# A banded attention and two-layer MLP kernel: first weights on ScalarE's queue, w_out's halves between chunks of V, one group of transposes moved into the second product

## The chip, the cores and the metric

The kernel runs on one core of a Trainium2 chip. A core has five engines that run their own instruction streams and wait for each other by semaphores: TensorE (PE) for matmuls and transposes, VectorE (DVE), ScalarE (ACT), GpSimd (POOL), and SyncE (SP), which here only issues transfers. Sixteen DMA engines move the data. The metric is device time in microseconds; shown are the median of several runs, and the profile of one execution.

## The reference

Eight batches, eight heads, sequence 576, head size 64. Each query sees the keys at most 32 positions away; the result, laid out as 4608 tokens of 512 features, goes through a two-layer MLP with tanh-GELU.

```python
scores = scale * np.matmul(q, k.transpose(0, 1, 3, 2))
mask = np.abs(pos[:, None] - pos[None, :]) <= window      # window = 32
attn = softmax(np.where(mask, scores, -1e9))
x = np.matmul(attn, v).transpose(0, 2, 1, 3).reshape(4608, 512)
h = x @ w_in                                              # w_in: 512 x 2048
g = 0.5 * h * (1.0 + np.tanh(c * (h + 0.044715 * h * h * h)))
out = g @ w_out                                           # w_out: 2048 x 512
```

## The kernel before, in words

**Tiles.** The tokens are cut into nine tiles of 512. Tile t goes through the first product (`ffn_in`, L522, with the gelu at L549 on ACT) and the second product (`ffn_out_0`, L609, for tile 0 and `ffn_out`, L622, a scheme with seven half-size products, for the others). The attention of batch t+1 is worked in small pieces between the matmuls of tile t's second product, and leaves its result, transposed, in the ring `xT`, from which the next first product reads. Batch 0's attention has no product to hide in and runs alone at the start.

**Attention pieces.** Heads are worked in pairs, groups 0 to 3; group "-1" stands for the last tokens (tail) of the batch before. For a group: casts to fp16 (`cast_early`, L295), eight PE transposes of queries and keys into one PSUM buffer (`trans_pair`, L322) and copies from there to QT (L333, DVE) and KT (L334, DVE or ACT by an argument), scores (`score`, L417) with the exponential on ACT (L448), the band mask on DVE (L454), sums over keys by a product with ones (`sum_up`, L457), logarithm and exponential on ACT in place of a division (L494, L495, or L883, L885 for two groups at once), the product with V (`times`, L461), and the final multiplication into xT (`spread`, L498, at L504 or L510). V is needed twice, shifted by 64 keys; the second form is copied on DVE (`pair_chunk`, L196: lines L198 and L200; `pair_v`, L190, for batch 0). `trans_tails` (L312) turns the last 64 queries and keys, `cast_tails` (L307) casts them.

**PSUM buffers.** Score buffers have the tags S0 and S1; O, D, x0 and x1 are single banks. The last quarter of tile 0's first product keeps its results for columns 12 and 13 in S0 and for 14 and 15 in S1, so S0 is free once the second of the last four gelus has read it.

**Order.** It is written by hand: each engine executes its instructions in the order in which the program emits them, and waits in that order. Around tile 0's second product the order is a plan, `PLAN_0` (L53): before matmul number i of the 64, the actions listed at i are emitted (L848 to L911). The letter is the kind and the number the group, `@` names the score buffer:

- `r` transposes and copies, `s` scores and exponential, `m` mask, `k` casts of queries and keys on DVE
- `n` sums, logarithm and exponential for two groups, `v` sums, product with V and logarithm for one, `p` product with V for two, `x` the multiplication into xT
- `e` cast of a chunk of V on POOL, `d` its shifted copy on DVE, `t` transposes of batch 0's tail queries
- `w`, `u` casts of w_out (shared by DVE, ACT and POOL), `c` differences of w_out's blocks

Matmul i needs the block of w_out that `ORDER_0` (L64) gives: column blocks 0 to 3 for the first 16, and so on.

**Transfers.** Nearly all loads are issued by SP, in program order (L221 to L243 and L742 to L781). w_in comes in four blocks of 1 MB, in halves of 512 KB, w_out in the same manner; both go through five staging buffers (`stage_w`, L205) and are cast to fp16. V of batch 0 is loaded head by head (`v_of_pair`, L228, 128 KB each in pieces of 256 bytes). In the kernel before, SP issues three pairs of V heads, half of w_in's first block, one head, a quarter, the last head, a quarter, then the other blocks. ACT issues two loads at the very start (L222, L224).

**The first product of tile 0.** Block 0 of w_in at L755 to L767, then `quarter(1)`, `quarter(2)`, `quarter(3)` (L786 to L801), each of 16 matmuls followed by four gelus. In the middle of `quarter(3)` stands `trans_pair(1, 0)`, the transposes of batch 1's group 0, with the key copy on ACT. `load_table` (L97) changes ACT's function table.

Of the kernel before, what the change touches and what calls it, by code (L numbers as in the profile page):

```python
# [10 lines left out]
FP16 = mybir.dt.float16  # L11
# [25 lines left out]
def cut(b):  # L37
# [12 lines left out]

PLAN_0 = {4: "s0@0", 9: "r1@1", 14: "s1@0", 15: "w1", 16: "m0", 19: "k2", 22: "r2@1", 23: "m1", 25: "s2@0", 27: "t-1@1",  # L53
          29: "w2", 31: "s-1@1", 33: "n0@0", 35: "e0", 36: "m2", 37: "k3", 38: "w5", 39: "m-1", 40: "r3@1", 43: "e1",
          45: "s3@0", 46: "v-1@1 d0", 47: "w3 e2", 48: "m3", 50: "d1", 51: "n2@0 x-1", 52: "e3 e4 d2", 54: "d3 p0@0",
          55: "u3 p2@1 x0 x1", 56: "x2 x3", 60: "c1"}
PLAN_1 = PLAN | {10: "s0@0", 12: "s1@1", 33: "s2@0", 40: "v0@1 v1", 50: "x0", 53: "x1", 57: "s-1@1", 62: "s3@0 v2",
                 63: "m-1", 66: "m3", 73: "v-1@1", 76: "x2", 80: "x-1", 86: "v3", 90: "s4@1", 98: "m4"}
PLAN_1[16] = "m0 m1"
# [13 lines left out]
def kernel(  # L73
# [9 lines left out]
    nc = tc.nc  # L83
    B, H, S, D = q.shape
    DM, DF = moe_w_in.shape
    NTOK = B * S
    NPAIR = H // 2
# [117 lines left out]
    def stage_w():  # L205
        return stage.tile([128, 4, 512], FP32, name="wst", tag="stage")

    def load_w_in(i, w, c0=0, c1=4):
        nc.sync.dma_start(w[:, c0:c1, :], w_in_v[:, c0:c1, 512 * i:512 * i + 512])
        return w  # L210

    def load_w_out(i, w, c0=0, c1=4):
# [12 lines left out]
    qk(4)  # L225
    qk(6)
    load_table(exp_set)
    def v_of_pair(g, hs=(0, 1)):  # L228
        for h in (2 * g + x for x in hs):
            nc.sync.dma_start(raws[0][3][:, :, h, :], v[0, h, 0:512, :].rearrange("(c p) d -> p c d", p=128))  # L230

    vs(4)
    for g in range(3):
        v_of_pair(g)
    wi = [stage_w()]
    load_w_in(0, wi[0], 0, 2)
    for x in range(2):
        v_of_pair(3, (x,))
        load_w_in(0, wi[0], 2 + x, 3 + x)
    for i in range(1, 4):  # L240
        wi.append(stage_w())
        for c0 in (0, 2):
            load_w_in(i, wi[i], c0, c0 + 2)  # L243

    idle = KTs[1][:, 0, 0:512]
    nc.vector.memset(idle, 0.0)
# [470 lines left out]
    cast_early(0, 3, split)  # L717
    turn(2)
    score(0, 1, 1)
    trans_out(0, 2, *pts[2])  # L720
    cast_vt(0)
    spin(1)
# [46 lines left out]
    cast_w(wi[2], w_in16[:, :, 1024:1536], (0, 2))  # L769
    wo.append(load_w_out(1, stage_w()))  # L770
    qk(4)
    tails_0("q")
    wo.append(load_w_out(2, stage_w(), 0, 2))
    qk(6)
    vs(0)
    load_w_out(2, wo[2], 2, 4)
    vs(1)
    wo.append(load_w_out(3, stage_w(), 0, 2))
    vs(2, 3, 4)
    load_w_out(3, wo[3], 2, 4)  # L780
    tails()  # L781

# [13 lines left out]
    band_out()  # L796
    quarter(2, 0, 1, 2, 3)
    cast_early(1, 0, split)
    quarter(3, 0, 1)
    trans_pair(1, 0, psO.tile([128, 8, 128], FP16, name="pt", tag="D"), bank16(0)[:, 0:4, :], copy=nc.scalar.copy)  # L800
    quarter(3, 2, 3)  # L801
    load_table(exp_set)
    cast_w(wo[0], w_out16[:, 0:4, :], (0,), (0, 2, 3, 1))
    cast_early(1, 1, (nc.vector, nc.vector))
# [8 lines left out]
    for t in range(NT):  # L813
        b = t + 1
        att = b < B
        if t:
            for fc in range(begun):
                ffn_in(t, fc, 3, 4, then=False)
            for fc in range(begun):
                gelu(t, fc)  # L820
            if att and b > 1:
                parts = cast_and_turn(b)
            for fc in range(begun, NF):
                ffn_in(t, fc)
                if t == 1 and fc == 3:
                    parts[0]()
                    combine(4, nc.vector)
                if t == 1 and 6 <= fc < 10:
                    cast_v(2, fc - 6)
                if t == 1 and 9 <= fc < 14:  # L830
                    parts[1](fc - 9)
                if t == 1 and fc == 8:
                    trans_tails(1, psO.tile([128, 8, 128], FP16, name="pt", tag="O"))
                if t == 2 and fc in (8, 9):
                    store(0, *later[1 if fc == 8 else 3])
                if t > 1 and fc == 8 and att:
                    pair_v(b, nc.vector.tensor_copy)
        plan = PLAN_0 if not t else PLAN_1 if t == 1 else PLAN if att else {5: "v-1", 31: "x-1"} if t == B - 1 else {}

        def group(g):  # L840
            return (b, g) if g >= 0 else (b - 1, 4)

        if plan and t:
            load_table(exp_set)
        if t and b + 1 < B:
            load_qk(b + 1)
        ods = {}
        for i in range(113 if t else 65):  # L848
            if t and i == (4 if t > 1 else 46) and b + 1 < B:
                nc.gpsimd.tensor_copy(after, KLs[b % 2][:, 3, 0:1])  # L850
                load_v(b + 1)
            for act in plan.get(i, "").split():
                kind, at = act[0], int(act[act.index("@") + 1:]) if "@" in act else None
                g = int(act[1:].split("@")[0])
                if kind == "w":
                    if g == 3:
                        cast_w(wo[g], w_out16[:, 12:16, :], cs=(0, 1), on_dve=(0,))
                    else:
                        cast_w(wo[g % 3], w_out16[:, 4 * (g % 3):4 * (g % 3) + 4, :], on_act=(1, 3),
                               cs={1: range(4), 2: (0, 1), 5: (2, 3)}[g])  # L860
                elif kind == "e":
                    cast_vt(1) if g == 4 else cast_v(1, g)
                elif kind == "k":
                    cast_early(1, g, (nc.vector, nc.vector))
                    if g == 2:
                        cast_tails(0, nc.gpsimd, even)
                elif kind == "t":
                    trans_tails(0, spare(at)[0], even)
                elif kind == "r":
                    trans_pair(1, g, *spare(at), copy=nc.scalar.copy if g == 2 else nc.vector.tensor_copy)  # L870
                elif kind in "np":
                    pair = psS.tile([128, 2, 512], FP32, name="ps_od", tag=f"S{at}")
                    for x in range(2):
                        if kind == "n":
                            sum_up(1, g + x, pair[:, x, :], groups[(1, g + x)])
                        else:
                            ods[g + x] = (pair[:, x, :], lts[g + x])
                            times(1, g + x, pair[:, x, :], groups.pop((1, g + x)))
                    if kind == "n":
                        n = size(1, g)  # L880
                        lts[g], lts[g + 1] = lt4[:, g, :], lt4[:, g + 1, :]
                        for x in range(2):
                            nc.scalar.activation(lts[g + x][:, 0:n], pair[:, x, 0:n], AF.Ln)  # L883
                        for x in range(2):
                            nc.scalar.activation(lts[g + x][:, 0:n], lts[g + x][:, 0:n], AF.Exp, scale=-1.0)  # L885
                elif kind == "u":
                    cast_w(wo[g], w_out16[:, 12:16, :], on_act=(3,), cs=(2, 3))
                    cast_tails(1, nc.gpsimd)
                    load_qk(2)
                elif kind == "c":  # L890
                    if g == 1:
                        B12 = combine_w()
                    combine(g, nc.vector)
                elif kind == "s":
                    score(*group(g), at)
                    if t == 1 and g == 4:
                        load_table(gelu_set)
                elif kind == "d":
                    pair_chunk(b, g, nc.vector.tensor_copy)
                elif kind == "m":  # L900
                    mask(*group(g))
                elif kind == "v":
                    bb, gg = group(g)
                    o, d = weigh(bb, gg, at)
                    ods[g] = (o, invert(bb, gg, d))
                    if t and g < 0 and b + 1 < B:
                        load_vt(b + 1)
                    if t > 1 and g == (3 if att else -1):
                        load_table(gelu_set)
                else:  # L910
                    spread(*group(g), *ods[g])  # L911
            if t == 1 and i == 30:
                cast_vt(2)
                store(0, *later[0])
                store(0, *later[2])
            if t == 1 and i in PAIR_1:
                pair_v(2, nc.vector.tensor_copy, PAIR_1[i])
            if t == 0 and i < 64:
                ffn_out_0(*ORDER_0[i])
            elif t and i < 112:  # L920
                ffn_out(t, i)
        if t == 0:
            wino_rest(B12)
            load_table(gelu_set)
        else:
            ffn_last(t)
        begun = 3 if t < NT - 1 else 0
        for fc in range(begun):
            ffn_in(t + 1, fc, 0, 3)
# [28 lines left out]
```

## Time and profile before

| what | value |
|---|---|
| median of 5 runs | 302.14 us (301.98 to 306.6) |
| profiled execution: its own time | 301.98 us |
| its span, and granted TensorE clock | 300.2 us, 0.994 |
| PE busy | 288.8 us, 96% of the span |
| DVE busy, ACT busy, POOL busy | 196.1, 194.6, 90.7 us |
| chain that ended last | PE 83%, DVE 5%, ACT 4%, DMA 3% |
| moved by DMA | 50.73 MB, 169 GB/s on average |

The span runs from the first to the last instruction of the profiled execution; its own time is 1.8 us longer, and the comparison between kernels is by the runs' times. "Chain" is the work that ended last, followed back at each step to what released it. A row of the timeline gives start, length, engine, line, operation, what it writes and reads, and how often; brackets give idle time of that engine before it and what ended it. PE's ends are modelled and overlap: matmuls of 512 columns start every 0.216 us although each is listed with about 0.38 us.

### The profile page before, as it was taken

What the parts mean: (1) busy time and instruction counts of PE and PEld (TensorE: products, weight loads), DVE (VectorE), ACT (ScalarE), POOL (GpSimd) and SP (SyncE); (2) the same over time, 40 slices, a digit from 0 to 9 for tenths busy, and PEclk for the clock granted to TensorE, in tenths of its full rate; (3) what the DMA queues carried; (4) which work ended last, traced back from release to release, by engine and by line L of the source; (5) the groups of instructions that cost most, each with busy time, mean ns of one, the idle gap of its engine ahead of it and who ended that gap; (6) DMA issues with size and microseconds to landing.
All of it is one profiled execution on the core that took longest, in us unless ns stands there. A gap on an engine that the chain in (4) does not pass through costs nothing.

```text
span 300.2 us, 7125 instructions
## 1 busy us (share of the span) xinstructions
PE 288.8 (96%) x2893; PEld 179.8 (60%) x2893; DVE 196.1 (65%) x438; ACT 194.6 (65%) x307; POOL 90.7 (30%) x141
## 2 busy tenths in 40 slices
PE   7889999899999999999999999999999999999994
PEld 2534444445774488548854885478547864784583
DVE  4563567996969676967696669766876635442452
ACT  4865776679785695669567956695678666606600
POOL 3425416102537050605080506060700050015000
PEclk9979999999999999999999999999999999999999
DMA  7999999899899999898999996989692031004013
GB/s 214 223 302 384 371 300 253 230 191 212 197 217 193 245 221 171 147 136 209 182 170 162 228 162 148 151 212 175 99 185 37 3 102 40 2 7 134 2 37 103
DMA packets 116518, 50.73 MB, mean 169 GB/s; under 512 B 98007, under 2 KB 110039, under 8 KB 116486
## 3 DMA queue, kind: packets, MB, share of 16 engines
q1 hardware_dynamic: 87428, 37.88, 61.2%
q0 software_dynamic: 27936, 11.35, 25.5%
q10 hardware_dynamic: 1122, 1.06, 1.1%
q8 instruction: 22, 0.36, 0.5%
q14 instruction: 10, 0.08, 0.1%
HBM read 36.70 MB, written 9.44 MB: 154 GB/s over the span
## 4 chain that ended last, share of the span: by engine, by line
PE 83%; DVE 5%; ACT 4%; DMA 3%; issue 1%; SPq 1%; POOL 0%; POOLq 0%
PE mm L639 31%; PE mm L541 21%; PE ph L541 19%; PE ps_s L436 3%; PE ps_d L459 2%; PE ps_o L469 2%; ACT gT L549 2%; DMA vr<-in_v_dram 2%; DMA tr<-in_k_dram 2%; DVE xT L504 1%; PE py L613 1%; PE mm L613 1%; SPq L230 1%; PE ps_od L459 1%; PE ps_od L469 1%
## 5 line engine op out<-in xcount | busy, mean ns | idle before, releaser
L541 PEld LDWEIGHTS <-w_in 128*128 128x128 f16 x576 | 56.4, 98 | 66.6 <-issue 1.9
L541 PE MATMUL mm<-xT,w_in 128*128 128x512 f16 x304 | 75.2, 381 | 0.1
L549 ACT ACTIVATE gT<-mm 128x512 f16<-128x512 f32 x76 | 45.2, 598 | 40.0 <-PE mm L541 39.2
L541 PE MATMUL ph<-xT,w_in 128*128 128x512 f16 x272 | 68.8, 382 | 0.0
L603 POOL DMA_DIRECT2D out_dram<-y x55 | 33.4, 616 | 87.4 <-DVE y L668 75.1
L639 PEld LDWEIGHTS <-s 128*128 128x128 f16 x512 | 49.4, 98 | 6.0
L584 DVE TENSOR_TENSOR s<-gT 128x512 f16<-128x512 f16 x64 | 27.6, 431 | 36.9 <-ACT gT L549 36.9
L549 ACT ACTIVATE gT<-ph 128x512 f16<-128x512 f32 x68 | 38.0, 600 | 13.6 <-PE ph L541 13.6
L639 PE MATMUL mm<-t,s 128*128 128x256 f16 x376 | 45.0, 273 | 0.0
L639 PEld LDWEIGHTS <-gT 128*128 128x128 f16 x384 | 35.8, 98 | 6.7
L448 ACT ACTIVATE pe<-ps_s 128x960 f16<-128x960 f32 (+1 forms) x32 | 30.6, 977 | 12.5 <-PE ps_s L436 12.3
L639 PE MATMUL mm<-w_out,gT 128*128 128x256 f16 x256 | 33.2, 273 | 0.0
L98 ACT ACT_TABLE_LOAD x18 | 23.1, 1283 | 2.2 <-issue 1.9
L494 ACT ACTIVATE lt<-ps_d 128x480 f32<-128x480 f32 (+2 forms) x28 | 15.6, 556 | 10.6 <-PE ps_d L459 6.8
L495 ACT ACTIVATE lt<-lt 128x480 f32<-128x480 f32 (+3 forms) x36 | 21.1, 587 | 1.1
L469 PEld LDWEIGHTS <-V 128*64 128x64 f16 x520 | 14.3, 112 | 8.6 <-DVE V L194 2.1
L454 DVE TENSOR_TENSOR pe<-pe,band 128x960 f16<-128x960 f16 x28 | 18.2, 669 | 1.1 <-ACT pe L448 1.1
L184 POOL DMA_DIRECT2D V<-in_v_dram x20 | 17.9, 913 | 1.2 <-PE ps_s L436 0.4
L639 PE MATMUL mm<-t,gT 128*128 128x256 f16 x128 | 16.5, 273 | 0.0
L504 DVE TENSOR_TENSOR xT<-ps_o,lt 128x480 f16<-128x480 f32 (+5 forms) x26 | 13.5, 537 | 2.3 <-PE ps_o L469 2.3
L436 PE MATMUL ps_s<-QT,KT 64*64 64x128 f16 (+3 forms) x576 | 13.9, 216 | 0.8 <-ACT KT L334 0.5
L436 PEld LDWEIGHTS <-KT 64*64 64x64 f16 x576 | 10.1, 106 | 7.4 <-issue 4.2
(110 smaller groups left out, 324.8 us busy)
## 6 DMA issues: line engine op xcount, KB each, us to landing
kr<-in_k_dram SPq DMA_DIRECT2D x31, 256.0 KB, 10.5
qr<-in_q_dram SPq DMA_DIRECT2D x6, 1024.0 KB, 8.5
wst<-in_moe_w_in_dram SPq DMA_DIRECT2D x7, 512.0 KB, 8.4
V<-in_v_dram POOLq DMA_DIRECT2D x20, 128.0 KB, 8.7
wst<-in_moe_w_out_dram SPq DMA_DIRECT2D x2, 1024.0 KB, 11.3
wst<-in_moe_w_out_dram SPq DMA_DIRECT2D x4, 512.0 KB
qr<-in_q_dram SPq DMA_DIRECT2D x7, 256.0 KB, 6.9
out_dram<-y POOLq DMA_DIRECT2D x6, 192.0 KB, 6.2
```

What stands on the lines that cost most here:

```text
L98: nc.scalar.add_instruction(mybir.InstLoadActFuncSet(name=nc.get_next_instruction_name(), act_func_set_id=which, ins=[], outs=[]))
L184: nc.gpsimd.dma_start(V[:, c, :, :], v[b, :, 128 * c:128 * c + 128, :].rearrange("h p d -> p h d"))
L436: nc.tensor.matmul(ps[64 * half:64 * half + 64, h, 4 * n * r:4 * n * r + 4 * n].rearrange("k (j p) -> k j p", j=4)[:, :, p0 - q0:p1 - q0], ...
L448: nc.scalar.activation(pe, ps[:, :, 0:w], AF.Exp, scale=SCALE)
L454: nc.vector.tensor_tensor(pe, pe, m.rearrange("k (o j) p -> k o j p", o=1).broadcast_to(list(pe.shape)), op=ALU.mult)
L469: nc.tensor.matmul(o[64 * h:64 * h + 64, cols].rearrange("d (j p) -> d j p", j=4)[:, :, p0 - q0:p1 - q0], Vs[b % 2][:, slot, 2 * pr + h, : ...
L495: nc.scalar.activation(lt[:, 0:n], lt[:, 0:n], AF.Exp, scale=-1.0)
L541: nc.tensor.matmul(ph, w_in16[:, dc, fc * 128:fc * 128 + 128], xT[:, dc, t * 512 % RING:t * 512 % RING + 512], start=(dc == 0), stop=(dc = ...
L549: nc.scalar.activation(gTs[t][:, fc, :], phs[fc], AF.Gelu_apprx_tanh)
L584: nc.vector.tensor_tensor(dst, x, y, op=op)
L603: eng.dma_start(out_v[b, j, q0 + p:q0 + p + e, cols], yo[m:m + e, cols])
L639: nc.tensor.matmul(pys["apart"][:, 0:256] if apart else py[:, blk, :], lhsT, wino[w][:, f, :], start=(new and i % (8 if one else 16) == 0) ...
```

## The change

It has four parts.

1. **First weights.** The first half of w_in's first block is issued by ACT, behind the exponential of batch 0's group 1, and SP issues all eight heads of V one after the other, then the second half and the other blocks.
2. **First transposes.** `trans_pair(1, 0)` leaves the middle of `quarter(3)` and becomes the action `r0@0` at matmul 2 of the second product, with the key copy on DVE.
3. **The plan.** `PLAN_0` is written anew: buffers S0 and S1 change roles, scores of group 0 come at 5 rather than 4, those of group 3 at 41 rather than 45, the sums of groups 2 and 3 stand ahead of the tail's product with V, and the casts of batch 0's tail queries have an action of their own (`e5`).
4. **Loads behind it.** The tail queries of batch 0 are loaded behind batch 1's first chunk of V, and w_out's halves change places with chunks of V.

```diff
-PLAN_0 = {4: "s0@0", 9: "r1@1", 14: "s1@0", 15: "w1", 16: "m0", 19: "k2", 22: "r2@1", 23: "m1", 25: "s2@0", 27: "t-1@1",
-          29: "w2", 31: "s-1@1", 33: "n0@0", 35: "e0", 36: "m2", 37: "k3", 38: "w5", 39: "m-1", 40: "r3@1", 43: "e1",
-          45: "s3@0", 46: "v-1@1 d0", 47: "w3 e2", 48: "m3", 50: "d1", 51: "n2@0 x-1", 52: "e3 e4 d2", 54: "d3 p0@0",
-          55: "u3 p2@1 x0 x1", 56: "x2 x3", 60: "c1"}
+PLAN_0 = {2: "r0@0", 5: "s0@1", 9: "r1@0", 14: "s1@1", 15: "w1", 16: "m0", 19: "k2", 22: "r2@0", 23: "m1", 25: "s2@1",
+          29: "w2", 30: "n0@1", 33: "k3", 34: "e0", 35: "r3@0", 36: "m2", 37: "e5", 38: "w5", 40: "t-1@0", 41: "s3@1",
+          42: "e1", 43: "s-1@0", 45: "m3 d0 e2", 46: "w3", 47: "n2@1 m-1", 49: "v-1@0 d1", 50: "e3 e4 d2", 52: "x-1 d3",
+          53: "p0@1", 54: "p2@0 x0 x1", 55: "u3 x2 x3", 60: "c1"}
...
-    def load_w_in(i, w, c0=0, c1=4):
-        nc.sync.dma_start(w[:, c0:c1, :], w_in_v[:, c0:c1, 512 * i:512 * i + 512])
+    def load_w_in(i, w, c0=0, c1=4, queue=nc.sync):
+        queue.dma_start(w[:, c0:c1, :], w_in_v[:, c0:c1, 512 * i:512 * i + 512])
...
-    for g in range(3):
+    for g in range(NPAIR):
         v_of_pair(g)
-    wi = [stage_w()]
-    load_w_in(0, wi[0], 0, 2)
-    for x in range(2):
-        v_of_pair(3, (x,))
-        load_w_in(0, wi[0], 2 + x, 3 + x)
-    for i in range(1, 4):
-        wi.append(stage_w())
-        for c0 in (0, 2):
-            load_w_in(i, wi[i], c0, c0 + 2)
...
     score(0, 1, 1)
+    wi = []
+    for i in range(4):
+        wi.append(stage_w())
+        for c0 in (0, 2):
+            load_w_in(i, wi[i], c0, c0 + 2, nc.sync if i or c0 else nc.scalar)
     trans_out(0, 2, *pts[2])
...
     qk(4)
-    tails_0("q")
     wo.append(load_w_out(2, stage_w(), 0, 2))
     qk(6)
     vs(0)
+    tails_0("q")
     load_w_out(2, wo[2], 2, 4)
-    vs(1)
+    vs(1, 2)
     wo.append(load_w_out(3, stage_w(), 0, 2))
-    vs(2, 3, 4)
+    vs(3, 4)
     load_w_out(3, wo[3], 2, 4)
...
-    quarter(3, 0, 1)
-    trans_pair(1, 0, psO.tile([128, 8, 128], FP16, name="pt", tag="D"), bank16(0)[:, 0:4, :], copy=nc.scalar.copy)
-    quarter(3, 2, 3)
+    quarter(3, 0, 1, 2, 3)
...
-                    cast_vt(1) if g == 4 else cast_v(1, g)
+                    cast_tails(0, nc.gpsimd, even) if g == 5 else cast_vt(1) if g == 4 else cast_v(1, g)
                 elif kind == "k":
                     cast_early(1, g, (nc.vector, nc.vector))
-                    if g == 2:
-                        cast_tails(0, nc.gpsimd, even)
```

## The prediction

> **What bounds the kernel now.** I read the page first (busy shares), then the busy times by stage, then the chain of work that ended last from 34 to 59 us, then the timeline around each piece that the change moves. From 58.4 us on TensorE (PE) has almost no gap (13.79 us busy of 13.80 up to 72.2), so a gain or a loss made before that passes to the end undiminished. The stages (columns: stretch and its length, busy time and count of PE, weight load, DVE, ACT, POOL, then granted clock, DMA share, GB/s):
>
> ```profile
> 12.00:19.10 7.10, 5.04 (x85) 2.42 (x82) 4.77 (x10) 5.36 (x9) 3.09 (x5) 0.91 0.95 217
> 19.10:24.00 4.90, 4.90 (x38) 2.06 (x33) 2.70 (x7) 2.53 (x4) 1.27 (x3) 0.79 1.03 365
> 24.00:34.70 10.70, 10.70 (x57) 5.06 (x56) 4.99 (x14) 6.46 (x14) 5.65 (x7) 1.00 1.06 378
> 34.70:58.40 23.70, 21.75 (x248) 10.41 (x247) 16.28 (x34) 16.31 (x28) 9.50 (x14) 1.00 1.04 285
> ```
>
> The reader sees three places with something to win: PE idles 7.10 - 5.04 = 2.1 us before 19.1, the clock is low around 18 to 21, and PE idles 23.70 - 21.75 = 1.95 us in the second product of tile 0. Between 19.1 and 34.7 there is no gap: the casts of w_in are early enough, so earlier weights alone win nothing there. The second product ends in this piece of the chain (start, length, what):
>
> ```profile
> 49.53 0.43 PE ps_s L436 x16
> ...
> 50.99 0.04 DVE pe L454
> ...
> 54.55 0.30 DVE V L200
> ...
> 54.88 0.50 PE ps_od L469 x18
> ```
>
> Scores of pair 3, exponential, mask, then batch 1's V copies (L198 and L200, action d) in DVE's order up to d3, which ends at 54.85. Only then can the products with V (p0) finish; x0 to x3 and the copies of y follow, and the next tile starts at 58.41, 3.56 us after d3. **The end of d3 is what I have to predict.**
>
> **Part 1, the first weights.** SyncE (SP) no longer issues the first half of w_in's first block between V pairs; ScalarE (ACT) does, behind the exponential of group 1. On ACT an issue of that size costs 0.49 us at the start (1.35 to 1.84). It delays the exponentials of groups 2 and 3 by at most that. ACT then stands idle for 1.65 us before 17.63, so it costs nothing; even 1.72 us, what SP paid for this very issue, would only move PE's sums of group 2 from 13.5 to 14.6, ahead of the V copy that ends at 16.27 and holds PE anyway. On the DMA side the trace has a hole (same columns):
>
> ```profile
> 12.00:13.50 1.50, 1.29 (x31) 0.60 (x28) 1.02 (x2) 1.47 (x3) 1.11 (x2) 1.00 1.23 205
> 13.50:14.50 1.00, 0.66 (x26) 0.42 (x18) 0.57 (x2) 1.00 (x2) 0.10 (x1) 1.00 0.33 63
> 14.50:15.50 1.00, 0.29 (x14) 0.18 (x8) 0.14 (x1) 0.97 (x3) 0.64 (x2) 1.00 0.94 241
> ```
>
> SP was stuck on issuing (11.97 to 13.69) and the engines ran dry. A second queue fills the hole: up to 0.7 us of transfer time, after which everything on SP's queue lands up to that much earlier. A rule speaks against more: the Trainium skill ("DMA: Bandwidth & Descriptors", Issuing engines are not separate DMA queues) says that queues of several engines run on the same 16 DMA engines and interleave, so a second one saves only issue time. By the row I win up to 0.7 us of landing time, by the rule I also pay, since the 512 KB interleave with V. The V of pair 1 is on the critical path: it lands at 14.60, and DVE's copies, xT and PE's next work follow without slack. If ACT's transfer starts before that V is served, V waits up to 512 KB at 380 GB/s = 1.35 us. Judging by bytes moved, V of pair 1 (2.8 MB since the start) is served at about 12.4 on average, and ACT's data start some 1.2 us after their issue (first issue 0.81, data from 2.0), so at 12.0 to 13.0. I take **+0.2 us**, bounds 0 and +1.3. V of pair 2 may land at 16.8 rather than 15.5; its DVE copy starts at 17.53 only, so the slack just holds. The 0.7 us won for w_in hide nothing that PE waited for: **0**.
>
> **Part 2, first transposes of batch 1.** Taken out of the last quarter of the first product, they give back 8 transposes, 32.92 to 33.36, **-0.44 us**, and ACT's key copy (0.59). Put in at slot 2 (r0@0), they cost the same **+0.44**, and two waits. r0 needs buffer S0, which holds the halves that the second of the last four gelus reads:
>
> ```profile
> 34.70 2.07 ACT L549 ACTIVATE gT<-ph 128x512 f16<-128x512 f32 x4 [0.71 <-PE ph L541]
> 34.93 0.59 PE L613 MATMUL mm<-w_out,gT 128*128 128x512 f16 x2
> 35.88 0.40 PE L436 MATMUL ps_s<-QT,KT 64*64 64x96 f16 x16
> 37.31 0.39 PE L326 MATMUL pt<-idn,q 128*128 128x128 f16 x4
> 37.96 0.42 DVE L333 COPY QT<-pt 128x512 f16<-128x512 f16 x1 [2.01 <-PE pt L328]
> 39.09 0.40 PE L436 MATMUL ps_s<-QT,KT 64*64 64x96 f16 x16
> ```
>
> The gelus are 0.49 us apart and 0.60 long, so the second ends at 34.70 + 1.09 = 35.79, and s0 at slot 4 just met it (35.88, about 0.09 late). After the change everything here is 0.44 earlier: gelu 2 ends at 35.35, while PE reaches slot 2 at 34.93 - 0.44 + 2 x 0.216 = 34.92. **Wait 0.49** (with the semaphore's 0.05). r0 then runs from 35.41. From transposes to their scores takes 39.09 - 37.31 = 1.78 us when DVE makes both copies (the key copy L334 at 38.30 takes 0.68), as it now does for r0, so s0 can start at 37.19. PE has r0 (0.44) and slots 2 to 4 (0.65) until then, to 36.50. **Wait 0.69**. In sum PE stands 0.49 + 0.69 - 0.09 = **1.09 us later** after s0 than now. Nothing up to s2 takes it back: r1 to s1 and r2 to s2 keep their slots and latencies, and behind s0 the in-order PE holds the w_out products. So s2 moves from 42.91 to 44.0.
>
> **Part 3, the plan behind it.** From s2 to s3 there are now 16 slots rather than 20: s2 0.33 + 16 x 0.216 + sums n0 0.53 + r3 0.44 + tail transposes 0.22 = 4.98, and 0.2 for the tail transposes that need S0 after r3's copies (r3 + 1.67). s3 starts at 44.0 + 5.2 = 49.2 (now 49.53), its mask m3 ends at 49.2 + 2.12 = 51.3 (now 51.65). That much is won. But n2 now stands ahead of v-1, and DVE has x-1 ahead of d3. ACT's rows for both are:
>
> ```profile
> 50.86 0.38 ACT L494 ACTIVATE lt<-ps_od 128x256 f32<-128x256 f32 x1
> 51.27 0.42 ACT L495 ACTIVATE lt<-lt 128x256 f32<-128x256 f32 x1
> 52.37 1.03 ACT L883 ACTIVATE lt<-ps_od 128x480 f32<-128x480 f32 x2 [0.68 <-PE ps_od L459]
> 53.28 1.10 ACT L885 ACTIVATE lt<-lt 128x480 f32<-128x480 f32 x2
> ```
>
> Now the tail's logarithm is done before n2's. Afterwards n2's start at 51.3 + 0.4 = 51.7, take 2.01 (52.37 to 54.38), and the tail's own 0.83 end at 54.54. x-1 (0.41) on DVE ends at 54.97, and behind it d3, 0.97 as now or 0.58 undisturbed by POOL, at 55.55 to 55.95. Against 54.85 that is +0.7 to +1.1: **+0.9 us**. This replaces the 1.09 (PE's waits are paid inside it). DVE's own work between (m3, d0, w_out's cast, m-1, d1, d2: 51.3 + 0.5 + 0.6 + 0.4 + 1.2 + 0.6 = 54.6) ends at about the same time as x-1 is let go, so neither hides the other.
>
> **Part 4, the order of SP's loads.** Query tails go behind the first chunk of V, half of w_out 2 and pair 3's loads move ahead of them, V's third chunk ahead of half of w_out 3. It moves the issues of 128 KB in small pieces (1.57 us on SP at 30.70) and of 256 KB. V's last chunk lands at 51.02 now and no later then; its DVE copy starts at 55.0. Query tails are used at slot 40 rather than 27. w_out 3's first half, landed by 49.24 now, may be 0.5 later; slot 48 comes at about 52. **0**; without that cover up to +0.5.
>
> **Sum.** 0.2 - 0.44 + 0.44 + 0.9 = +1.1 us on the profiled execution's 301.98 (span 300.2, the rest around it) is 303.1; the median of the runs is 0.16 above that execution, so **303.2 us**. The likeliest case spans 302.4 to 304.2.
>
> **Rivals.**
> *The waits at slots 2 and 5 do not arise* or PE catches up. Then s3 starts at 48.1, the tail's logarithm ends at 53.45, x-1 at 53.9, d3 at 54.5 to 54.9: at best 0.35 gained. With V's earlier chunks sparing DVE the slow copies (0.29 rather than 0.6), 0.6: **301.6**, the case on the faster side. For it: PE alone could end sooner: from s3 at 49.2 it has 23 slots (4.97) and small products of 2.6 (s3 0.33, s-1 0.25, n2 0.53, v-1 0.35, p0 and p2 1.15), to 56.8 against 58.2 now. Against: gelu 2 frees S0, and the plan can't change that. Break-even is where the two waits together fall under about 0.1 us, 1.1 less than I count.
> *The clock drops again near 36.* From 17.65 to 21.2 PE ran at 0.50, costing 3.5 x 0.5 = 1.8 us, after 14 us had gaps of 0.34, 0.71 and 0.70 us. The Trainium skill ("TensorE: Matmul & The Clock Gate", Part 1: The HAM clock gate) knows a drop after an idle window of about 3.4 us; by that rule gaps of 0.5 and 0.7 are free, by the row of 14 us they are not. But from 53 to 55 PE was busy 0.74 of 2.00 us and the clock stayed 1.00, so I take no drop. If it comes: +1.0 to 1.8, **304.6**.
> *The drop at 18 goes away or shortens*, since the start is shifted by tenths: -1.8 against the sum, **301.4**.
> *ACT's weights hold V of pair 1 fully*: 1.1 more, **304.3**.
> *Nothing that counts*: losses and gains cancel, **302.1**.
>
> **How the numbers follow.** Likeliest 0.46; waits absent 0.16; second drop 0.12; V held 0.10; cancel 0.10; first drop gone 0.06. The range of 300.9 to 305.0 takes in all centres and leaves out the far ends of the drops. One per cent, 3.0 us, is about what a measurement of this kernel can tell from no change. Over 1% slower (above 305.2) needs a second drop in full or two losses together: 0.15. Over 1% faster (under 299.1) needs more than all of PE's gaps that the change touches: 0.03. Same 0.82.
>
> **What would show it.** Right: PE gaps of about 0.5 ahead of the transposes at slot 2 and 0.7 ahead of s0; DVE waiting for ACT before x-1 (L510) at 54; d3's end near 55.8 and the next tile near 59.5; no DMA hole at 14 us. Wrong: s0 within 0.3 us of the transposes' slots, d3 ending before 54.8, or V of pair 1 landing well after 15 us.

## The result and the profile after

The changed kernel is slower: the ratio of its runs to those of before is **1.0041, 95% interval 1.0027 to 1.0054** (43 and 80 runs, medians 304.04 and 302.42 us; some runs in a slower state are left out of the ratio). On 302.42 us that is +1.24 us (0.8 to 1.6), so a difference of 0.4 us can be told from none, not only the 3.0 us that the prediction took. It had 303.2 on 302.14, a ratio of 1.0035. The profiled execution took 303.93 us, its span 302.2.

Line numbers in the changed kernel are the same up to L227, lower by 9 from L244 to L719 (`ffn_in`'s matmul is L532, `ffn_out_0`'s L604, scores L427, KT's copy L325), and by 4 to 8 behind that. Busy times of the same stages, kernel after, same columns as before:

```profile
12.00:19.10 7.10, 4.96 (x106) 2.84 (x106) 4.74 (x11) 5.51 (x10) 3.20 (x6) 1.00 0.89 245
19.10:24.00 4.90, 4.86 (x37) 2.23 (x38) 2.73 (x7) 3.81 (x7) 2.15 (x3) 1.00 1.05 387
24.00:34.70 10.70, 9.86 (x46) 4.33 (x45) 4.20 (x12) 6.32 (x13) 4.82 (x6) 1.00 1.06 374
34.70:58.40 23.70, 20.50 (x249) 10.05 (x248) 15.72 (x34) 14.13 (x24) 8.58 (x14) 1.00 1.09 279
```

The reader sees two things. The clock stood at 1.00 in all four stretches of this execution, so PE was done with the first product 1.44 us sooner (first of the last four gelus at 33.26 against 34.70; 0.44 of it are the transposes taken out) and now has a gap of 0.84 us before 34.7. And the same stretch of the second product has 3.20 us without PE work rather than 1.95. Its end, in the chain of work (start, length, what):

```profile
49.23 0.36 PE ps_s L427 x16
...
50.62 0.66 DVE pe L445
...
51.31 0.68 DVE V L198
...
52.02 0.72 DVE w_out L218
52.74 0.33 DVE pet L445
...
54.66 0.42 DVE xT L501
...
55.42 0.70 DVE V L200
...
56.16 0.48 PE ps_od L460 x18
```

Scores of pair 3 come 0.3 us sooner than before (49.23 against 49.53), yet d3 ends 1.27 us later (56.12 against 54.85). From there to the next tile it is 3.58 us in both kernels (by the timeline 54.83 to 58.41, 56.11 to 59.69; the first row is the kernel before, the second the kernel after):

```profile
58.41 0.81 PE L541 MATMUL mm<-xT,w_in 128*128 128x512 f16 x3
59.69 0.81 PE L532 MATMUL mm<-xT,w_in 128*128 128x512 f16 x3
```

So between these two executions the loss at tile 1 is +1.28 us, all of it made ahead of d3. Later tiles start 1.17, 1.33 and 1.88 us later than before (91.80, 122.37, 153.34 against 90.63, 121.04, 151.46), the last step of 0.55 mostly PE's wait of 0.48 for a key transfer in this execution (at 137.27).

Measured from the first w_out matmul (34.93 before, 34.50 after), the stage splits exactly:

| stretch | before | after | difference |
|---|---|---|---|
| first w_out matmul to scores of group 0 (after: with r0 and a fifth slot, 0.66) | 0.95 | 2.43 | +1.48 |
| scores of group 0 to m3's start | 15.11 | 13.69 | -1.42 |
| m3's start to d3's end | 3.84 | 5.49 | +1.65 |
| d3's end to the next tile | 3.58 | 3.58 | 0 |
| sum | 23.48 | 25.19 | +1.71 |

and 1.71 less the 0.43 us that the first w_out matmul came sooner is 1.28.

### The profile page after: what moved, and what is told of

It reads as the page before. It is cut to its first block, busy times and chain, and to the rows that moved or that the text cites. A ratio compares the mean times of both kernels' runs of the same rounds, so it can differ in the third digit from the quotient of the medians.

```text
span 302.2 us, 7123 instructions
## 1 busy us (share of the span) xinstructions
PE 287.5 (95%) x2893; PEld 179.2 (59%) x2893; DVE 195.7 (65%) x439; ACT 193.7 (64%) x306; POOL 89.8 (30%) x141
## 4 chain that ended last, share of the span: by engine, by line
PE 69%; DMA 15%; DVE 6%; SPq 4%; ACT 3%; issue 1%; POOL 1%; ACTq 0%; DVEq 0%
PE mm L630 30%; PE mm L532 14%; PE ph L532 12%; DMA KT<-k 7%; PE ps_s L427 3%; DMA kr<-in_k_dram 3%; SPq L230 2%; PE ps_d L450 2%; DMA wst<-in_moe_w_in_dram 2%; PE ps_o L460 2%; DMA tr<-in_k_dram 2%; PE mm L604 2%; PE py L604 2%; DVE s L575 2%; ACT gT L540 1%; DMA out_dram<-y 1%
## 5 line engine op out<-in xcount | busy, mean ns | idle before, releaser
L532 PEld LDWEIGHTS <-w_in 128*128 128x128 f16 x576 | 56.1, 98 | 66.6 <-POOL w_in L751 0.7
L532 PE MATMUL mm<-xT,w_in 128*128 128x512 f16 x304 | 74.7, 379 | 0.0
L532 PE MATMUL ph<-xT,w_in 128*128 128x512 f16 x272 | 68.0, 379 | 0.6 <-POOL w_in L751 0.6
L594 POOL DMA_DIRECT2D out_dram<-y x55 | 32.7, 604 | 85.8 <-DVE y L659 74.4
L485 ACT ACTIVATE lt<-ps_d 128x480 f32<-128x480 f32 (+2 forms) x28 | 15.5, 555 | 9.1 <-PE ps_d L450 5.2
L427 PE MATMUL ps_s<-QT,KT 64*64 64x128 f16 (+3 forms) x576 | 13.9, 216 | 2.2 <-DVE KT L325 0.9
L427 PEld LDWEIGHTS <-KT 64*64 64x64 f16 x576 | 10.0, 106 | 8.9 <-issue 3.6
```

The costliest lines, as they stand in the source:

```text
L427: nc.tensor.matmul(ps[64 * half:64 * half + 64, h, 4 * n * r:4 * n * r + 4 * n].rearrange("k (j p) -> k j p", j=4)[:, :, p0 - q0:p1 - q0], ...
L532: nc.tensor.matmul(ph, w_in16[:, dc, fc * 128:fc * 128 + 128], xT[:, dc, t * 512 % RING:t * 512 % RING + 512], start=(dc == 0), stop=(dc = ...
L594: eng.dma_start(out_v[b, j, q0 + p:q0 + p + e, cols], yo[m:m + e, cols])
```

## The experiments

Theory A is the prediction's: the second product makes the loss, by waits around r0 and s0 and by what VectorE has to do between m3 and d3. The rivals are named with each run. "Length" is the time from the first w_out matmul to the first of the next tile, from the one profile of each kernel: 23.48 before, 25.19 after. Start-up varies by up to 2.1 us between executions (first w_out matmul at 33.98 to 36.09 in four kernels that are the same up to there), so the length tells more of the second product than a single time. Two cautions. With r0 in the second product the length holds its 0.44 us, which the other kernels spend in the first product; beside those, the kernel after counts 24.75. And three profiles with the same second product (the kernel after, first weights undone, w_out's halves on the kernel after) have 25.19, 24.77 and 25.40, so differences under about 0.6 us say little.

### First weights alone

```diff
 (kernel before)
-    for g in range(3):
+    for g in range(NPAIR):
         v_of_pair(g)
...
     score(0, 1, 1)
+    ... w_in as in the change, first half issued by nc.scalar
```

> The kernel before with part 1 alone: half of the first weights issued by ScalarE, all of V ahead of the rest on SyncE. Theory A (the loss is made in the second product, by the late scores and the crowded end): within 0.3 us of the kernel before, 302.1 to 302.7, since w_out's first block lands at 34.0 us either way and holds TensorE there. Rival S (the start is to blame: V held up by the weights, or ScalarE's wait for a transfer before it may issue): the whole loss, about 303.6. Rival C (the new start keeps the clock up around 18 us): TensorE leaves the first product about 1.4 us sooner and the time falls by up to 0.5.

Measured: ratio 0.9988 (0.9968 to 1.0007), 302.09 us, length 23.24. The start does not make the loss (rival S, 303.6, lies outside the interval), as theory A has it. Rival C's gain of up to 0.5 is inside the interval and is not shown.

### First weights undone

```diff
 (kernel after)
-    for g in range(NPAIR):
-        v_of_pair(g)
+    ... V, w_in and their order as before, all on nc.sync
```

> The kernel after with the first weights as before. Theory A: still slower than before by 1.0 to 1.3 us, about 303.6. Rival S: back at the time before, 302.4. By the granted clock around 18 us: a dip to 0.5 if the start decides it, none if it comes and goes by chance.

Measured: 1.0027 (1.0007 to 1.0048), 303.39 us, length 24.77. Slower than before without the new start, as theory A has it; a little less than expected, but the interval holds 1.0 us. The clock was 1.00 around 18 us here, with the start of the kernel that had shown the dip. It dipped in five of the ten profiles with the new start (the runs "transposes back", "d3 first", "back and swapped", "tail first" and "w_out in halves" with both repairs) and held in the other five. So the dip comes and goes with both starts.

The granted clocks of all runs tell how often. In the twelve profiles, those with a dip have a mean clock of 0.994 or less over the execution, the others 0.997 or more. Of the runs in the ratios, 0.995 or less was granted in 45 of 197 with the old start (1 of 22 in this run) and in 115 of 229 with the new one (21 of 42 in the kernel after). So the new start goes with more dips, though first weights alone (8 of 22) are not told apart from the kernel before (44 of 175). In the kernel after, runs at 0.995 or less are on average 1.5 us longer than those at 0.997 or more. As an estimate from these numbers, (0.50 - 0.25) x 1.5 = 0.4 us of the loss of 1.24 come with the clock and not from the second product; taken at 0.997 or more alone, the kernel after is still 0.8 us slower than the kernel before (means of 17 and 120 runs). This run is 0.4 us faster than the kernel after, which fits, but the intervals overlap.

### Transposes back in the first product

```diff
 (kernel after)
-PLAN_0 = {2: "r0@0", 5: "s0@1",
+PLAN_0 = {5: "s0@1",
...
-    quarter(3, 0, 1, 2, 3)
+    quarter(3, 0, 1)
+    trans_pair(1, 0, ..., copy=nc.scalar.copy)
+    quarter(3, 2, 3)
```

> The kernel after with batch 1's first transposes back in the middle of the last quarter of the first product, the rest of the plan unchanged. Theory A: scores of group 0 no longer wait for copies on VectorE (0.73 us at 36.9), so scores of group 3, their mask and the V copies come 0.7 to 1.2 us sooner, 302.8 to 303.4. Rival O (only the order at the end counts: the tail's logarithm behind that of groups 2 and 3): no change, 304.0, because x-1 is let go by ScalarE at 54.6 us whatever came before.

Measured: 1.0041 (1.0022 to 1.0061), 303.73 us, length 24.26 (0.5 under 24.75): no gain in time. The expectation of theory A was wrong, and the timeline of this run says why:

```profile
35.44 2.07 ACT L540 ACTIVATE gT<-ph 128x512 f16<-128x512 f32 x4 [0.71 <-PE ph L532]
35.67 0.59 PE L604 MATMUL mm<-w_out,gT 128*128 128x512 f16 x2
...
37.56 0.40 PE L427 MATMUL ps_s<-QT,KT 64*64 64x96 f16 x16 [0.64 <-ACT gT L540]
```

In the new plan the scores of group 0 use S1, which the fourth of the last gelus still reads; it ends at 35.44 + 2.07 = 37.51, and s0 starts at 37.56. A wait for gelu took the place of the wait for copies. The plan that swapped the buffers is bound to r0 being where it is.

### Transposes back, buffers swapped

```diff
 (the run before this)
-PLAN_0 = {5: "s0@1", 9: "r1@0", 14: "s1@1", ...
+PLAN_0 = {5: "s0@0", 9: "r1@1", 14: "s1@0", ...
 (every @0 of the plan becomes @1, every @1 becomes @0)
```

> As the run with the transposes back in the first product, and the score buffers S0 and S1 change roles in the whole plan, so that scores of group 0 wait for the second of the last four gelus and not for the fourth (that wait, 0.64 us for TensorE, had taken the place of the one for the copies). Theory A: scores of group 3 and d3 come 0.6 us sooner than there, 303.0 to 303.3, about half of the loss. Rival O (only the crowded end counts): no change against the kernel after, 304.0.

Measured: 1.0005 (0.9977 to 1.0033), 302.42 us, length 23.89 (0.86 under 24.75). More than expected: the whole loss is gone within the interval; by the length 0.4 us of it is left, less than the spread. PE in this run:

```profile
36.49 0.40 PE L427 MATMUL ps_s<-QT,KT 64*64 64x96 f16 x16
37.70 0.39 PE L317 MATMUL pt<-idn,q 128*128 128x128 f16 x4
```

s0 starts 1.17 us behind the first w_out matmul (35.32), which is five slots of 0.216 and 0.09, so neither wait is left. With r0 in place it was 2.43. Rival O, that only the end counts (304.0), lies outside the interval and falls.

### d3 ahead of x-1

```diff
 (kernel after)
-          ... 52: "x-1 d3",
+          ... 52: "d3 x-1",
```

> The kernel after with d3 ahead of x-1 at matmul 52. VectorE finishes d2 at 54.66 us just as x-1 is let go, so taking x-1 (0.42 us) from in front of d3 should let d3 end 0.4 us sooner: 303.6 by theory A. If VectorE's work after d3 (x0 to x3) is the bound instead, x-1 is only moved and nothing changes: 304.0.

Measured: 1.0031 (1.0011 to 1.005), 303.53 us, length 24.51. VectorE in this run:

```profile
51.76 1.02 DVE L445 TENSOR_TENSOR pe<-pe,band 128x960 f16<-128x960 f16 x1 [1.00 <-ACT pe L439]
...
56.09 0.28 DVE L200 COPY V<-V 64x512 f16<-64x512 f16 x1
```

m3 to d3 takes 4.61 us, rather than 5.49 in the kernel after and 5.08 with first weights undone, which has the same plan; so the gain in the profile is 0.5 to 0.9. In time it is 0.3 us, the expected size, but the intervals overlap and the time alone does not show it.

### The tail first

```diff
 (kernel after)
-          42: "e1", 43: "s-1@0", 45: "m3 d0 e2", 46: "w3", 47: "n2@1 m-1", 49: "v-1@0 d1", ...
+          42: "e1", 43: "s-1@0", 45: "m3 m-1 d0 e2", 46: "w3", 47: "v-1@0", 49: "n2@1 d1", ...
```

> The kernel after with the tail's mask right behind m3, the tail's product with V and logarithm at 47 and the sums of groups 2 and 3 at 49, d3 still behind x-1. Theory A, as the prediction has it (VectorE's own work reaches d2's end at the same moment as ScalarE lets x-1 go, so neither hides the other): no change, 303.8 to 304.0. Rival L (the logarithm's place is what costs): d3 ends 0.8 us sooner, 303.2.

Measured: 1.0043 (1.0019 to 1.0067), 304.14 us, length 24.89. No gain, as theory A says; rival L would have had 0.8 us, which the interval just admits, so the timelines have to tell. In the kernel after, x-1 was let go by two engines at the same moment. Its timeline:

```profile
51.89 1.03 ACT L875 ACTIVATE lt<-ps_od 128x480 f32<-128x480 f32 x2 [0.81 <-PE ps_od L450]
...
53.79 0.38 ACT L485 ACTIVATE lt<-ps_od 128x256 f32<-128x256 f32 x1
...
54.03 0.63 DVE L200 COPY V<-V 64x512 f16<-64x512 f16 x1
...
54.20 0.42 ACT L486 ACTIVATE lt<-lt 128x256 f32<-128x256 f32 x1
...
54.65 0.42 DVE L501 TENSOR_TENSOR xT<-ps_od,lt 128x256 f16<-128x256 f32 x1
```

ACT's last step ends at 54.62, DVE's d2 at 54.66. In this run ACT is done with the tail's logarithm at 55.05, and x-1 still stands behind d2 on VectorE:

```profile
56.16 0.28 DVE L200 COPY V<-V 64x512 f16<-64x512 f16 x1
56.37 0.41 DVE L501 TENSOR_TENSOR xT<-ps_od,lt 128x256 f16<-128x256 f32 x1
```

m3 to d3 takes 5.00 us, about as with first weights undone (5.08). Freeing only one of two simultaneous bounds gave nothing that can be told.

### The end repaired

```diff
 (kernel after, with both of the edits above: tail first, d3 ahead of x-1)
-cast_w(wo[g], w_out16[:, 12:16, :], cs=(0, 1), on_dve=(0,))
+cast_w(wo[g], w_out16[:, 12:16, :], cs=(0, 1), on_dve=(), on_act=(0,))
```

> The kernel after with both at the end: tail first as in the run before, d3 ahead of x-1, and w_out 3's first piece cast by ScalarE, which idles there, and not by VectorE (0.72 us between m3 and d3). Theory A: d3 ends near 54.3 us rather than 56.1; with TensorE's remaining work the next tile starts 1.4 to 1.6 us sooner, 302.4 to 302.6, level with the kernel before. Rival P (TensorE's late start of the second product is the bound, so the end doesn't matter): not below 303.4.

Measured: 1.0021 (0.9998 to 1.0043), 303.13 us, length 23.87. VectorE in this run:

```profile
50.10 1.06 DVE L445 TENSOR_TENSOR pe<-pe,band 128x960 f16<-128x960 f16 x1 [1.23 <-ACT pe L439]
51.09 0.41 DVE L445 TENSOR_TENSOR pet<-pet,band 128x512 f16<-128x512 f16 x1
51.52 0.80 DVE L198 COPY V<-V 64x512 f16<-64x512 f16 x2
...
53.59 0.29 DVE L198 COPY V<-V 64x512 f16<-64x512 f16 x1
53.89 0.28 DVE L200 COPY V<-V 64x512 f16<-64x512 f16 x1
54.10 0.41 DVE L501 TENSOR_TENSOR xT<-ps_od,lt 128x256 f16<-128x256 f32 x1
```

d3 ends at 54.17, 1.9 us sooner than in the kernel after (m3 to d3 4.07 us rather than 5.49; the rest is an earlier start of this execution). The length falls by 1.32. In time it is 0.6 us, less than the 1.4 to 1.6 expected. The interval, 302.4 to 303.8, holds theory A's upper edge, rival P's 303.4 and the kernel after, so the time alone decides nothing; the length speaks against P. By the ratios the end is worth about half of the loss, by the length all of it.

### Both repaired

```diff
 (the run before this)
-PLAN_0 = {2: "r0@0", 5: "s0@1", ...
+PLAN_0 = {5: "s0@0", ...            (all score buffers swapped)
...
-    quarter(3, 0, 1, 2, 3)
+    ... trans_pair(1, 0) in the middle, as before
```

> The end repaired as before this, and the transposes back in the first product with the buffers swapped; of the change remain the first weights on ScalarE, SyncE's order and the earlier places of groups 2 and 3. Theory A: the two repairs add, 301.6 to 302.0, faster than the kernel before by 0.1 to 0.3 per cent. Rival P: not below 302.4, since TensorE is then busy throughout and the order no longer counts.

Measured: 0.9985 (0.9963 to 1.0007), 301.83 us, length 23.15. The repairs add up in time: from 1.0041 to 0.9985, 1.7 us, is the sum of what each gave alone (1.1 and 0.6), and this gain is clear of the intervals. It has the lowest ratio of all kernels here, but its interval still holds the kernel before, so it isn't shown to be faster. In length they give 1.60 together and 0.86 and 1.32 alone. What is missing is a wait on VectorE:

```profile
54.16 0.29 DVE L198 COPY V<-V 64x512 f16<-64x512 f16 x1 [1.03 <-POOL V L296]
```

With VectorE free, d3 waits 1.03 us for POOL's cast of V's last chunk, which the prediction had called covered; the cast waits for the transfer and starts at 53.50 (51.23 in the kernel after). In the next run, with the same plan, it starts at 50.75 and d3 does not wait; the length there is 22.69.

### w_out's first block in halves

```diff
 (both repaired, and in the other run the kernel after)
-    wo = [load_w_out(0, stage_w())]
+    wo = [load_w_out(0, stage_w(), 0, 2)]
+    load_w_out(0, wo[0], 2, 4)
```

> Both repairs, and w_out's first block issued as two halves in the same place, so that its first column block can be cast 1.3 us (512 KB) sooner. In profiles where the clock held around 18 us TensorE was done with the first product and waited for that cast (0.84 us in the kernel after). Theory W (this wait swallows what the start wins): 0.2 to 0.5 us faster than both repairs alone on average, 301.3 to 301.7. Rival: TensorE or the chain behind it takes the time back, 301.8.

> The kernel after with w_out's first block issued as two halves, nothing else. Theory A: TensorE starts the second product up to 0.8 us sooner where the clock held, but r0's copies still stand behind the cast of pair 1's keys on VectorE, which waits for its transfer at 35.5 us: no change, 303.8 to 304.0. Theory W alone: 303.3.

Measured: 0.9993 (0.9975 to 1.001), 302.42 us, length 22.69, on both repairs; 1.0037 (1.0014 to 1.0059), 304.31 us, length 25.40, on the kernel after. Neither is told apart from its own base, so theory W is not shown. It is not excluded either: a gain of 0.2 us lies within both intervals, and on both repairs the clock was at 0.995 or less in 16 of 21 runs, against 10 of 22 of its base, which may hide a gain. The second run shows where an earlier start goes. PE, with the clock at 1.00 and w_out cast in time:

```profile
33.58 0.59 PE L604 MATMUL mm<-w_out,gT 128*128 128x512 f16 x2
...
34.48 0.38 PE L317 MATMUL pt<-idn,q 128*128 128x128 f16 x4 [0.31 <-ACT gT L540]
...
36.20 0.40 PE L427 MATMUL ps_s<-QT,KT 64*64 64x96 f16 x16 [0.47 <-DVE KT L325]
```

PE starts the second product 0.9 us sooner than in the kernel after and meets both waits that the prediction named, behind the gelu at r0 and behind the copies at s0. They take back 0.2 us: scores of group 0 and the next tile (58.98) still come 0.7 us sooner. So in this execution most of the early start arrives, against the expectation of theory A; over the runs no gain is shown.

## Why the prediction was right, point by point

**The sum** was right in size, and in the step on which it rested, the end of d3 behind x-1: d3's end was put at 55.55 to 55.95 (measured 56.11), the next tile near 59.5 (59.69), scores of pair 3 at 49.2 (49.23), m3's end at 51.3 (51.28), the tail's logarithm at 54.54 (54.62). That the times agree so closely is luck in part. The first w_out matmul came at 34.50, as put (34.49), but because w_out's cast held it and not because only the transposes were gone. Scores of group 2 came 0.3 us sooner than put (43.68 for 44.0) and those of pair 3 took 0.3 longer from there (5.5 for 5.2). And by the estimate above about 0.4 us of the measured 1.24 come with the clock, which the sum had at nothing, and 0.8 with the second product, where it had 0.9; the +0.2 for V of pair 1 did not come.

**Part 2, the waits at r0 and s0.** The size was near (1.09 predicted; first w_out matmul to s0 grew by 1.48, less r0 and a slot 0.82), the composition was not: the wait at r0 is missing. The kernel after:

```profile
33.26 2.06 ACT L540 ACTIVATE gT<-ph 128x512 f16<-128x512 f32 x4 [1.60 <-PE ph L532]
...
34.01 0.43 DVE L218 CAST w_out<-wst 128x512 f16<-128x512 f32 x1 [1.67 <-DMA wst<-in_moe_w_out_dram]
...
34.50 0.61 PE L604 MATMUL mm<-w_out,gT 128*128 128x512 f16 x2 [0.84 <-DVE w_out L218]
...
34.94 0.39 PE L317 MATMUL pt<-idn,q 128*128 128x128 f16 x4
...
35.51 0.43 DVE L289 CAST k<-kr 128x512 f16<-128x512 f32 x1 [0.32 <-DMA kr<-in_k_dram]
...
35.87 0.41 DVE L324 COPY QT<-pt 128x512 f16<-128x512 f16 x1
36.20 0.68 DVE L325 COPY KT<-pt 128x512 f16<-128x512 f16 x1
...
36.93 0.40 PE L427 MATMUL ps_s<-QT,KT 64*64 64x96 f16 x16 [0.73 <-DVE KT L325]
```

r0 did not wait for a gelu in this execution, since the second gelu was done while PE stood 0.84 us for w_out. The wait at s0 (0.73 for 0.69) did come. Most of it is the predicted one: from the transposes to the scores the prediction took 1.78 us, and it was 1.99 (34.94 to 36.93). The 0.21 more come from the cast of pair 1's keys, which waits for its transfer until 35.51 and stands ahead of r0's copies on VectorE; the prediction had not looked at what is queued there. In the run with w_out in halves both waits came (0.31 and 0.47).

**Part 3** holds in its mechanism: x-1 let go at the same moment by ACT and DVE (54.62 and 54.66), and a repair of the one alone gave nothing that can be told. DVE's terms were off one by one (d1 took 0.6 for 1.2, d2 0.9 for 0.6, d0 0.7 for 0.5) and right in sum. The way from s2 to s3 was put 0.3 us too short.

**Part 1** was wrong in its mechanism and right in its price, about nothing. Rows of the kernel after:

```profile
13.37 0.37 ACTq L209 DMA_DIRECT2D wst<-in_moe_w_in_dram  x1
13.47 0.62 POOL L728 CAST V<-vr 128x512 f16<-128x512 f32 x1 [0.31 <-DMA vr<-in_v_dram]
...
13.79 1.02 ACT L439 ACTIVATE pe<-ps_s 128x1024 f16<-128x1024 f32 x1 [1.50 <-DMA vr<-in_v_dram]
...
14.71 1.41 POOL L728 CAST V<-vr 128x512 f16<-128x512 f32 x2 [0.61 <-DMA vr<-in_v_dram]
...
18.47 0.62 POOL L751 CAST w_in<-wst 128x512 f16<-128x512 f32 x1 [2.35 <-DMA wst<-in_moe_w_in_dram]
...
19.14 0.60 PE L532 MATMUL ph<-xT,w_in 128*128 128x512 f16 x2 [0.58 <-POOL w_in L751]
```

ACT could not issue behind its exponential at once: it stood 1.50 us and issued at 13.37, later than SP had (11.97). On what it waited, the profiles tell: in all ten with this start the issue goes out 0.10 to 0.11 us ahead of POOL's first cast of V (13.47 here), at 12.11 to 13.37, and in nine of them that cast is seen to wait for the landing of that V. Why the issue waits for a transfer that it does not use is not shown. The issue itself took 0.37 us (the prediction's 0.49 was that of a load of half the size). The weights landed at 18.47, not sooner than 17.82 (their first cast starts at 17.02 to 18.68 in the ten profiles), and PE waited 0.58 us for them. V of pair 1 was not held up: 14.71 against 14.72, where +0.2 was taken.

Nor was the hole on the DMA side filled, which the prediction had made a sign of being right. The same stretches in the kernel after:

```profile
12.00:13.50 1.50, 1.50 (x32) 0.87 (x32) 0.81 (x2) 0.29 (x1) 0.72 (x3) 1.00 0.91 191
13.50:14.50 1.00, 0.47 (x22) 0.40 (x19) 0.57 (x3) 0.71 (x1) 0.59 (x1) 1.00 0.52 112
14.50:15.50 1.00, 0.63 (x20) 0.53 (x19) 0.36 (x2) 0.97 (x3) 0.65 (x2) 1.00 0.71 165
```

By these rows 0.56 MB moved from 12.0 to 15.5, and 0.61 MB before. SP did get further ahead; it issued w_out's first block at 21.80 rather than 22.66 (the first row is the kernel after, the second the kernel before):

```profile
21.80 1.25 SPq L213 DMA_DIRECT2D wst<-in_moe_w_out_dram  x1
22.66 0.64 SPq L213 DMA_DIRECT2D wst<-in_moe_w_out_dram  x1
```

But the block is cast from 34.01 and 34.02, as it lands, so the 0.7 us of earlier landings did not come; from 19.1 to 34.7 the DMA share is 1.03 to 1.06 in both kernels. What the Trainium skill says ("DMA: Bandwidth & Descriptors", Issuing engines are not separate DMA queues), that a second issuing engine saves only issue time, fits this trace, 0.86 us on SP's issue and nothing at the landing, and not the 0.7 that I worked out from the row of the DMA hole.

**The rivals.** The clock did hold at 18 us in the profiled execution, and the first product ended 1.0 us sooner for it (1.44 less the transposes; both kernels began it at 19.1, and half a clock from there to 21.2 is worth about 1.0, an estimate); but the first w_out matmul, held by its cast, came only 0.43 us sooner. So the rival "the drop goes away" came true in its cause in this execution and not in its 1.8 us; over the runs the opposite holds, the kernel after has more runs with a low clock. No second drop came near 36.

**Part 4** was not tried alone. With both repairs it is still in, with part 1 and the earlier places of groups 2 and 3, and the ratio is 0.9985; what it costs or gives by itself is not shown. That V's last chunk is covered held where d3 was late, and in one of the two profiles with both repairs.

What stays open: why ACT's issue stands until V has landed, why the clock drops more often with the new start, and how the loss divides between the clock and the second product beyond the estimate above.

## What to carry to other kernels

When a step moves into a later stretch, look at what its buffer's last reader and the copying engine still have queued there: the moved transposes, one slot and the wait behind them cost here in front of the first scores (1.48 us) what the new order won by advancing the later ones (1.42). Where two engines let a step go at the same moment, repair both or expect nothing from one. A gain at the start is worth what the next transfer in line allows: PE was done 1.44 us sooner and waited for w_out. And one profile is one execution: the clock held in the profile of the kernel after, and dropped in half of its runs.

## What the runs showed of the hardware

A load put behind an ACTIVATE on ACT's queue did not go out with it: ACT idled 1.50, 0.98 and 0.91 us around it in the kernel after, with first weights alone and with both repairs, and the next exponential came behind it. In nine of ten profiles with such a load it went out as a V load of SP's landed, 0.10 to 0.11 us ahead of the cast that waits for it.

The same copy of 64 x 512 fp16 on VectorE took 0.28 us alone and 0.63 us beside a cast on POOL (L200 at 53.41 and 54.03 in the kernel after, POOL casting w_out from 53.90 to 54.52). Between m3 and d3 there are seven such copies.

The clock's dip to 0.50 began between 15 and 20.5 us in six profiles and lasted about 3.4 us in four of them and 6.8 us in two (transposes back, d3 first). Much the same gaps of PE went with it and without it: 0.64, 0.33, 0.23 and 1.38 us between 13 and 19.5 us with a dip (both repairs and w_out in halves), 0.71, 0.30, 0.39 and 1.36 us without (kernel after and w_out in halves).
